# High parts of queries, keys and first weights fetched by casting DMAs on GpSimd instead of cast by ScalarE and VectorE

## The chip, the cores and the metric

The kernel runs on one core of a Trainium2 chip. The metric is the device time of one execution in microseconds (us). The engines are TensorE (PE, with its weight loads shown apart as PEld), VectorE (DVE), ScalarE (ACT), GpSimd (POOL) and SyncE (SP), which here only issues transfers.

## What is computed

Three layers follow one another; this is the reference cut to what matters.

```
# attention: q, k, v of [2, 8, 576, 64], f of [2, 8, 576]
scores = q @ k.T / 8 ; decay = cum[:, None] - cum[None, :]   # cum = cumsum(log f)
attn = softmax(where(causal, -1e9, scores + decay)) ; x = attn @ v     # x: [1152, 512]
# soft mixture of 8 experts with Sinkhorn-normalised P
out = sum_e P[:, e] * (relu(x @ w1[e]) @ w2[e])
# last layer
h = out @ w_in ; g = h * tanh(softplus(h)) ; result = g @ w_out
```

## The kernel before, in words

TensorE multiplies fp32r operands, which are rounded fp32. To keep precision, an operand is split into a high part (rounded to fp32r) and a low part (the fp32 value minus the high part), and a product is the sum of three matmuls: high by high, high by low, low by high.

**The attention stage.** The two batches have five query tiles each (ten tiles, `ti` 0 to 9), and each tile has four units of two heads (`pi` counts units, 0 to 39). The main loop runs over half-steps `s`; `pi = s // 2`, `a = s % 2`, and inside a tile `st` counts its units, so that a place in the loop is written `(st, a)`. What an engine does follows the order in which the loop emits it; nothing is reordered later. In a half-step come, in this order: the exponentials of the half-unit before (ACT), at `a = 1` the normalisation of the unit before (POOL, line 512), the scores of this half-unit (PE lines 468 and 469, then a masked reduction on DVE, line 481), a few warming matmuls, `fill()` (matmuls of the first expert once they are possible), at `a = 1` the product with v for the unit three back (PE line 568) and the transposes of the unit two back (PE lines 532 and 544), and then the preparation of the next tile.

**Preparation of the next tile (`prep`).** At `(0, 0)` the query tile `ti + 1` is split, at `(0, 1)` the key tile. Their four groups of transposes (PE line 361) are emitted at `(1, 0)`, `(1, 1)`, `(2, 0)` and `(2, 1)`, queries and keys in turn. The raw tile (`raw`, three buffers) was fetched by SP (`load_raw`, line 147) about a tile earlier. The split writes a tile `hl` (a ring of two buffers): high part by `split2` on ACT (line 317) or DVE (line 319), low part on DVE or POOL (line 321). Tile 1 has its `hl` inside `big`, the space that later holds the first expert's weights.

**The planner.** `pick` adds up costs per engine in `busy` and gives a piece of work to the engine that would be least loaded; POOL starts at 10000. Evictions from PSUM (`evac`, lines 307 to 313), the splits and the weight splits go by it.

**First weights.** At `pi = 7` SP starts to fetch the first half of the first expert (line 61); from `pi = 12` on one task a unit splits one of its eight 128x512 pieces: `split_w`, high part on ACT (line 325) or DVE (line 327), low part on DVE (line 329).

After the attention stage come the Sinkhorn steps, the experts and the last layer. The change touches nothing there.

Of the kernel before, what the change touches and what calls it, by code (L numbers as in the profile page):

```python
# [9 lines left out]
FR = mybir.dt.float32r  # L10
AF = mybir.ActivationFunctionType
ALU = mybir.AluOpType
# [4 lines left out]
B, H, S, D = 2, 8, 576, 64  # L17
# [9 lines left out]
QT = {  # L27
    0: [(0, 128), (128, 128), (256, 128), (384, 128), (512, 64)],
    1: [(0, 64), (64, 128), (192, 128), (320, 128), (448, 128)],
}  # L30
KTL = [(0, 128), (128, 128), (256, 128), (384, 128), (512, 64)]
# [7 lines left out]
def f(ap):  # L39
    return ap.bitcast(F32)  # L40
# [43 lines left out]
def attention_moe_kernel(  # L84
# [13 lines left out]
    nc = tc.nc  # L98
# [18 lines left out]
    first_w = {n: big[:, 2048 * i:2048 * (i + 1)] for i, n in enumerate(("w1h", "w1l", "w2h", "w2l"))}  # L117
# [11 lines left out]
    with ExitStack() as actx:  # L129
        ap1 = actx.enter_context(tc.tile_pool(name="ap1", bufs=1))  # L130
        rawp = actx.enter_context(tc.tile_pool(name="rawp", bufs=3))
        hlp = actx.enter_context(tc.tile_pool(name="hlp", bufs=2))
# [100 lines left out]
        def cumulate_b(lo, hi):  # L233
# [21 lines left out]
            out=mask, in_=mask, compare_op=ALU.is_ge, fill=NEG, base=512,  # L255
# [19 lines left out]
        def quads(t):  # L275
            return t.rearrange("p (u a) (z t) -> p u (a z) t", a=2, z=2)
# [19 lines left out]
        def spent(engine, ns):  # L296
            busy[engine] += ns

        def pick(**cost):
            e = min(cost, key=lambda k_: busy[k_] + cost[k_])  # L300
            busy[e] += cost[e]
            return e
# [12 lines left out]
        def split2(raw, hi, lo):  # L315
# [4 lines left out]
            eng = nc.vector if pick(dve=640, pool=1260) == "dve" else nc.gpsimd  # L320
            eng.tensor_tensor(out=lo, in0=raw, in1=f(hi), op=ALU.subtract)

        def split_w(raw, hi, lo):
            if pick(act=540, dve=360) == "act":
                nc.scalar.copy(out=hi, in_=raw)
            else:
                nc.vector.tensor_copy(out=hi, in_=raw)
            spent("dve", 640)
            nc.vector.tensor_tensor(out=lo, in0=raw, in1=f(hi), op=ALU.subtract)

        def duplicate(o, i):
            nc.sync.dma_start(out=f(o), in_=f(i))

        def prep(kind, b, i, slots):

            s0, n = QT[b][i] if kind == "q" else KTL[i]
            st = {}

            def split(half=None):
                if not half:  # L340
                    st["raw"] = raws.pop((kind, b, s0))
                    if (b, i) == (0, 1):
                        o = 1024 * (kind == "k")
                        st["hl"] = big[:, o:o + 1024].rearrange("p (h z d) -> p h z d", z=2, d=D)
                    else:
                        st["hl"] = hlp.tile([128, H, 2, D], FR, tag="hl", name="hl")
                raw, hl = st["raw"], st["hl"]
                hs = slice(0, H) if half is None else slice(4 * half, 4 * half + 4)
                z = 0 if kind == "q" else 1
                hi, lo = hl[:n, hs, z, :], hl[:n, hs, 1 - z, :]  # L350
                if half is None:
                    split2(raw[:n], hi, lo)
                else:
                    nc.scalar.copy(out=hi, in_=raw[:n, hs])
                    nc.vector.tensor_tensor(out=lo, in0=raw[:n, hs], in1=f(hi), op=ALU.subtract)

            def trans(g, early=False):
                hl = st["hl"]
                pt = ps_t.tile([128, 4, 128], FR, tag="pt", name="pt")
                for u in range(4):  # L360
                    nc.tensor.transpose(  # L361
                        out=pt[:, u, :n],
                        in_=hl[:n, 4 * g + u].rearrange("p a d -> p (a d)"),
                        identity=idr[:n, :n],
                    )
                hs = slice(4 * g, 4 * g + 4)
                pv = f(pt[:, :, :n])
                if kind == "q":
                    a_, b_ = qa[slots[g]], qb[slots[g]]
                    if n == 64:  # L370
                        evac(quads(a_)[:, :, 0:4:3], pv.rearrange("p (u z) t -> p u z t", z=2), 4 * n, 0.125)
                    else:
                        evac(a_[:, :, :n], pv, 4 * n, 0.125)
                    if early:
                        evac(b_[0:64, :, :n], pv[0:64], 4 * n, 0.125)
                    else:
                        duplicate(b_[0:64], a_[0:64])
                        if g:
                            cum_q(b, i, g, slots[g])
                else:  # L380
                    o = kbase[b] + s0
                    evac(kt[:, hs, o:o + n], pv, 4 * n)
                    if early:
                        evac(kb[0:64, hs, o:o + n], pv[64:128], 4 * n)
                    else:
                        duplicate(kb[0:64, hs, o:o + n], kt[64:128, hs, o:o + n])

            return split, trans
# [271 lines left out]
        tiles = [(b, i) for b in range(B) for i in range(len(QT[b]))]  # L660
        units = []
        for ti, (b, i) in enumerate(tiles):
            s0, n = QT[b][i]
# [39 lines left out]
        for s in range(2 * nu + 8):  # L703
            pi, a = divmod(s, 2)
            ti, st = divmod(pi, 4)
            live = pi < nu
            prepping = live and ti + 1 < len(tiles)
            if prepping and st == 0 and a == 0:
                (qs, qt_), (ks, kt_) = make_preps(ti + 1)
            if 1 <= s <= 2 * nu:  # L710
                expo(units[(s - 1) // 2], (s - 1) % 2)
            if a and 1 <= pi <= nu:
                normalize(units[pi - 1])
            if live:
                scores(units[pi], a)
            if s < 16:
                warm((2,2,2,2,2,2,2,2,1,1,1,1,1,1,1,1)[s])
            elif s in (17,19,21,25,27):
                warm_late(1)
            fill()  # L720
            fills += ready
            ready = []
            if a and 3 <= pi < nu + 3:
                w = units[pi - 3]
                attend(w)
                if w["h"] == H - 2 and w["ti"] in (2, 6, 9):
                    c = (2, 6, 9).index(w["ti"])
                    gates.append(c)
                    if c < 2:
                        ready.append(filler(c))  # L730
                elif gates:
                    logits.append(gate(gates.pop(0)))
            elif logits:
                gate_end(*logits.pop(0))
            if a and 2 <= pi < nu + 2:
                transposes(units[pi - 2])
            if first:
                first.pop(0)()
            if prepping:
                nb_, ni = tiles[ti + 1]  # L740
                if (st, a) == (0, 0):
                    if ti == 3:
                        pad(2)
                    elif ti == 4:
                        pad(1)
                    elif ti in (5, 6):
                        unpad(0 if ti == 5 else 2)
                    cum_q(nb_, ni, 0, (2 * ti + 2) % 3)
                    qs()
                elif (st, a) == (0, 1):  # L750
                    ks()
                    if ti:
                        next_loads(ti + 2)
                elif (st, a) == (1, 0):
                    qt_(0)
                elif (st, a) == (1, 1):
                    if ti == 3:
                        pad(0)
                    elif ti == 5:
                        unpad(1)  # L760
                    kt_(0)
                    load_v(nb_, ni)
                elif (st, a) == (2, 0):
                    qt_(1)
                elif (st, a) == (2, 1):
                    kt_(1)
            if late_rows and s >= 2:
                late_rows.pop(0)()
            if a:
                continue  # L770
            s = pi
            if s == 3:
                nc.gpsimd.tensor_copy(out=wgc[:, :, 0, :], in_=wg)
                nc.gpsimd.tensor_tensor(out=wgc[:, :, 1, :], in0=wg, in1=f(wgc[:, :, 0, :]), op=ALU.subtract)
            if s == 7:
                wts.load(0, 0, stage)
                wts.load(0, 1, stage)
            if s == 8:
                cum_k(1, 0, 256)
            if s == 22:  # L780
                cum_k(1, 256, 576)
            if s >= 12 and wtasks:
                wtasks.pop(0)()
# [399 lines left out]
    for g in range(NF):  # L1183
        half, gg = g // 4, g % 4
        ph = l1(half, gg, 2, ps_h)
        h = new_h()
# [374 lines left out]
    for n_, (c, kk) in enumerate((c, kk) for c in (1, 2) for kk in range(KD)):  # L1561
        b = TB[n_ % 2] if n_ > 3 else 5
# [20 lines left out]
    for u in range(12):  # L1583
        c, gg = divmod(u, 4)
        b = HB[u % 4]
# [192 lines left out]
    for p in range(13):  # L1778
# [10 lines left out]
        if p % 2 == 0 and p:  # L1789
            h, n = 17 + (p // 2 - 1) // 2, (p // 2 - 1) % 2  # L1790
# [94 lines left out]
```

## Time and profile before

| | |
|---|---|
| median of 3 runs | 1086.73 us (1086.53 to 1086.83) |
| the profiled execution | 1087.39 us |
| its span, first to last instruction | 1085.6 us |
| PE busy | 1078.3 us (99%) |
| DVE, ACT, POOL busy | 839.3, 542.3, 75.5 us |
| mean granted TensorE clock | 0.998 |

The busy time of PE includes matmuls that wait in its pipeline, so 99% does not say that PE is never late. Weight loads (964.5 us) and the chain of waits show more. POOL's busy time all lies in the first 160 us, which is the attention stage; transfers that an engine issues are not counted as busy.

### The profile page before, as it was taken

The page shows a single profiled execution, that of the slowest core. Times are in us where ns is not written, and L with a number is a line of the kernel's source. Part 1 is how long each engine was busy: PE and PEld are TensorE (multiplying, and loading weights), DVE is VectorE, ACT ScalarE, POOL GpSimd, SP SyncE. Part 2 cuts the span into 40 slices and gives each one's busy share as a digit, 9 for nine tenths or more (in the row PEclk, how much of TensorE's full clock was granted, in tenths as well). Part 3 has the DMA queues.
Part 4 walks back from the last instruction along what each step waited for, and adds up shares of the span by engine and source line. Part 5 has one row for each costly group of instructions (what it writes and reads, how often), then busy time and mean ns, then how long its engine had stood idle before and what let it go on. Part 6 is the DMA issues. An engine that isn't in the chain of part 4 may idle for free.

```text
span 1085.6 us, 18374 instructions
## 1 busy us (share of the span) xinstructions
PE 1078.3 (99%) x6838; PEld 964.5 (89%) x6838; DVE 839.3 (77%) x1891; ACT 542.3 (50%) x1287; POOL 75.5 (7%) x124
## 2 busy tenths in 40 slices
PE   9999999999999999999999999999999999999998
PEld 8788779998989899898989989899898989899997
DVE  7856647878797887977888796887977559788994
ACT  7756632354425243342624435253443458887881
POOL 6644420000000000000000000000000000000000
PEclk9999999999999999999999999999999999999999
DMA  6534202023241424425343342524322341161402
GB/s 147 140 93 105 74 21 78 1 98 102 94 145 68 151 78 150 136 89 155 99 154 96 119 149 95 158 85 146 124 96 83 129 155 42 65 207 60 162 1 88
DMA packets 103805, 114.98 MB, mean 106 GB/s; under 512 B 35236, under 2 KB 63860, under 8 KB 103716
## 3 DMA queue, kind: packets, MB, share of 16 engines
q1 hardware_dynamic: 103716, 113.81, 33.3%
q8 instruction: 54, 0.88, 0.3%
q14 instruction: 35, 0.29, 0.1%
HBM read 82.24 MB, written 27.07 MB: 101 GB/s over the span
## 4 chain that ended last, share of the span: by engine, by line
PE 97%; DVE 1%; ACT 0%; issue 0%; POOL 0%; DVEq 0%; POOLq 0%
PE bank L856 33%; PE bank L1266 29%; PE bank L1738 9%; PE bank L1648 4%; PE ph L826 3%; PE x L568 3%; PE spare L1648 2%; PE bank L1577 2%; PE pa L856 2%; PE pa L641 2%; PE ph L622 1%; PE sp L468 1%; PE pt L361 1%; PE pt L532 1%; PE wt L395 1%; PE sp L469 1%
## 5 line engine op out<-in xcount | busy, mean ns | idle before, releaser
L856 PE MATMUL bank<-w2h,big 128*128 128x512 f32 x924 | 296.7, 390 | 0.0
L856 PE MATMUL bank<-w2l,big 128*128 128x512 f32 x528 | 205.7, 390 | 0.0
L856 PEld LDWEIGHTS bank<-w2h,big 128*128 128x128 f32 x924 | 173.5, 188 | 36.0 <-DVE hid_b L834 0.2
L1295 ACT COPY snap<-bank 128x288 f32<-128x288 f32 x168 | 66.9, 398 | 167.5 <-PE bank L1266 165.2
L833 ACT ACTIVATE big<-c 128x288 fp32r<-128x288 f32 x168 | 75.1, 447 | 84.6 <-DVE c L1300 81.0
L856 PEld LDWEIGHTS bank<-w2l,big 128*128 128x128 f32 x528 | 99.1, 188 | 19.9
L834 DVE SCALAR_TENSOR_TENSOR big<-c,big 128x288 fp32r<-128x288 f32 x140 | 64.1, 458 | 56.8 <-ACT big L833 54.2
L1031 DVE SCALAR_TENSOR_TENSOR acc<-bank,P,acc 128x512 f32<-128x512 f32 x132 | 92.4, 747 | 15.7 <-PE bank L856 15.6
L1266 PE MATMUL bank<-tt,ss 128*128 128x288 f32 x672 | 103.0, 295 | 0.0
L1266 PE MATMUL bank<-xh,ss 128*128 128x288 f32 x448 | 102.7, 295 | 0.0
L1266 PEld LDWEIGHTS bank<-tt,ss 128*128 128x128 f32 x672 | 93.1, 188 | 0.2
L1300 DVE TENSOR_TENSOR c<-bank,snap 128x288 f32<-128x288 f32 x168 | 76.0, 452 | 18.7 <-PE bank L1266 18.5
L1012 ACT CAST hb<-da 128x512 fp32r<-128x512 f32 x38 | 23.8, 625 | 107.0 <-DVE da L987 95.9
L1266 PEld LDWEIGHTS bank<-xh,ss 128*128 128x128 f32 x448 | 76.4, 188 | 0.0
L1266 PE MATMUL bank<-xl,ss 128*128 128x288 f32 x224 | 66.1, 295 | 0.0
L1266 PE MATMUL bank<-xh,w1l 128*128 128x288 f32 x224 | 66.0, 295 | 0.0
L1266 PE MATMUL bank<-xl,w1h 128*128 128x288 f32 x224 | 65.9, 294 | 0.0
L1266 PE MATMUL bank<-xh,w1h 128*128 128x288 f32 x224 | 65.7, 293 | 0.0
L75 DVE TENSOR_TENSOR w2l<-stg,w2h 128x512 fp32r<-128x512 f32 x60 | 41.2, 690 | 13.6 <-ACT w2h L74 13.6
L856 PE MATMUL bank<-w2h,hid_b 128*128 128x512 f32 x132 | 51.4, 389 | 0.0
L512 POOL TENSOR_SCALAR p<-p,rs 128x256 f32<-128x256 f32 (+5 forms) x72 | 42.2, 596 | 65.7 <-DVE rs L508 44.5
L1266 PE MATMUL bank<-tt,w1h 128*128 128x288 f32 x224 | 46.0, 293 | 0.0
(314 smaller groups left out, 2464.0 us busy)
## 6 DMA issues: line engine op xcount, KB each, us to landing
stg<-in_moe_w_dram SPq DMA_DIRECT2D x64, 512.0 KB
wb<-w_in_b SPq DMA_DIRECT2D x42, 256.0 KB
raw<-in_moe_w_in_dram SPq DMA_DIRECT2D x16, 512.0 KB
raw<-in_moe_w_out_dram SPq DMA_DIRECT2D x16, 512.0 KB
w_in_b<-hb SPq DMA_DIRECT2D x18, 256.0 KB
w_out_h<-hb SPq DMA_DIRECT2D x16, 256.0 KB
w_out_l<-da SPq DMA_DIRECT2D x16, 256.0 KB
w_in_f<-da SPq DMA_DIRECT2D x12, 256.0 KB
```

Source lines behind the costliest of these rows:

```text
L75: (lo_engine or nc.vector).tensor_tensor(out=lo, in0=raw, in1=f(hi), op=ALU.subtract)
L512: nc.gpsimd.tensor_scalar(out=p[:n, a, :nk], in0=p[:n, a, :nk], scalar1=r[:n, a:a + 1], scalar2=1.0, op0=ALU.mult, op1=ALU.mult,)
L568: nc.tensor.matmul(out=x[64 * a:64 * a + 64, h // 2, :n], lhsT=vts[b, j][:w, h + a, :], rhs=pT[:w, 128 * j + 64 * a:128 * j + 64 * a + 64] ...
L833: nc.scalar.activation(out=hh, in_=ph, func=AF.Relu)
L834: nc.vector.scalar_tensor_tensor(out=hl, in0=ph, scalar=0.0, in1=f(hh), op0=ALU.max, op1=ALU.subtract)
L856: nc.tensor.matmul(out=pa, lhsT=a_[:, ts_], rhs=w[wn][ft_], start=(first and n == 0), stop=(last and n == 2),)
L1031: nc.vector.scalar_tensor_tensor(out=acc[t], in0=pa, scalar=P[:, t, e:e + 1], in1=acc[t], op0=ALU.mult, op1=ALU.add)
L1266: nc.tensor.matmul(out=by_chunk(out_) if len(v_.shape) == 3 else out_, lhsT=u, rhs=v_, start=first and m == 0, stop=m == 5, skip_group_che ...
L1295: nc.scalar.copy(out=t, in_=bank["x", g])
L1300: nc.vector.tensor_tensor(out=t, in0=bank[of, g], in1=snap[with_, g], op=ALU.add)
L1648: nc.tensor.matmul(out=out_, lhsT=a_(kk, pa), rhs=b_(kk, pb), start=first and q == 0, stop=q == 5, skip_group_check=True,)
L1738: nc.tensor.matmul(out=bk[b][:, cs], lhsT=a_[:, ts_], rhs=w[wn][i][:, cs], start=i == 0 and q == 0, stop=i == 3 and q == 2,)
```

## The change

For tiles 2 to 9 the high parts of queries and keys no longer come from the raw tile on chip. A transfer issued by GpSimd reads the same rows from device memory a second time and rounds them to fp32r on the way into `hl`. It is issued two tiles ahead: the query's at `(2, 1)` and the key's at `(3, 0)` of tile `ti` for tile `ti + 2`. The low part is still a subtraction at the old place. The first expert's first weights get their high parts likewise, by four GpSimd transfers at `pi` 4, 5, 6 and 7. The raw tiles are fetched as before.

```diff
+        def lo_half(raw, hi, lo):
+            eng = nc.vector if pick(dve=640, pool=1260) == "dve" else nc.gpsimd
+            eng.tensor_tensor(out=lo, in0=raw, in1=f(hi), op=ALU.subtract)
+
+        high = {}
+
+        def load_high(kind, ti):
+            b, i = tiles[ti]
+            s0, n = QT[b][i] if kind == "q" else KTL[i]
+            t = hlp.tile([128, H, 2, D], FR, tag="hl", name="hl")
+            nc.gpsimd.dma_start(
+                out=t[:n, :, 0 if kind == "q" else 1],
+                in_=(q if kind == "q" else k)[b, :, s0:s0 + n, :].rearrange("h p d -> p h d"),
+            )
+            high[kind, b, i] = t
+
+        def load_high_w(part):
+            kk = part % 2
+            src = w1[0, kk * 256:(kk + 1) * 256, :512] if part < 2 else w2[0, kk * 256:(kk + 1) * 256, :]
+            nc.gpsimd.dma_start(
+                out=first_w["w1h" if part < 2 else "w2h"][:, 1024 * kk:1024 * kk + 1024].rearrange("p (k n) -> p k n", k=2),
+                in_=src.rearrange("(k p) n -> p k n", p=128),
+            )
+
         def split_w(raw, hi, lo):
-            if pick(act=540, dve=360) == "act":
-                nc.scalar.copy(out=hi, in_=raw)
-            else:
-                nc.vector.tensor_copy(out=hi, in_=raw)
             spent("dve", 640)
             nc.vector.tensor_tensor(out=lo, in0=raw, in1=f(hi), op=ALU.subtract)
...
+                    elif (kind, b, i) in high:
+                        st["hl"] = high.pop((kind, b, i))
+                        lo_half(st["raw"][:n], st["hl"][:n, :, 0 if kind == "q" else 1], st["hl"][:n, :, 1 if kind == "q" else 0])
+                        return
...
+            if live and ti + 2 < len(tiles) and (st, a) in ((2, 1), (3, 0)):
+                load_high("k" if a == 0 else "q", ti + 2)
...
             s = pi
+            if 4 <= s < 8:
+                load_high_w((2, 3, 0, 1)[s - 4])
```

## Rows read from the trace of the kernel before

**Rows 1.** Windows: busy time per engine, clock, share and rate of transfers.

```profile
20.00:40.00 20.00, 19.69 (x187) 16.32 (x187) 15.79 (x59) 17.21 (x49) 11.57 (x20) 1.00 0.65 175
...
400.00:800.00 400.00, 400.00 (x2345) 362.60 (x2345) 329.45 (x652) 161.15 (x364) 0.00 (x0) 1.00 0.39 125
```

**Rows 2.** Chain that ended last, 26 to 50 us: start, length, what.

```profile
39.84 0.33 DVE hl L319
40.18 0.35 DVE big L327
...
40.55 1.65 DVE big L329
```

**Rows 3.** Waits of weight loads, 17 to 50 us: total, times, longest.

```profile
PEld pt L361 <- POOL hl L321: 1.3, 3, 0.6
PEld sp L468 <- DVE nmax L481: 1.0, 1, 1.0
```

**Rows 4.** Windows of 4 us; the granted clock is third from the end.

```profile
42.00:46.00 4.00, 3.08 (x32) 2.43 (x31) 3.48 (x12) 2.52 (x6) 2.40 (x3) 0.78 0.44 99
46.00:50.00 4.00, 4.00 (x42) 2.73 (x40) 2.87 (x10) 3.03 (x8) 2.33 (x5) 0.80 0.65 182
```

**Rows 5.** Groups by line, 17 to 116 us: busy us, mean ns, idle before.

```profile
L319 DVE CAST hl<-raw 128x512 fp32r<-128x512 f32 x9 | 7.3, 808 | 0.0
...
L327 DVE CAST big<-stg 128x512 fp32r<-128x512 f32 x4 | 1.7, 420 | 0.0
...
L325 ACT CAST big<-stg 128x512 fp32r<-128x512 f32 x4 | 2.5, 621 | 0.0
...
L317 ACT CAST hl<-raw 128x512 fp32r<-128x512 f32 x3 | 1.8, 612 | 0.0
```

**Rows 6.** POOL in order of time: start, length, idle before and its releaser.

```profile
16.34 0.72 POOL L512 TENSOR_SCALAR p<-p,rs 128x128 f32<-128x128 f32 x2 [1.43 <-DVE rs L508]
...
17.81 0.72 POOL L512 TENSOR_SCALAR p<-p,rs 128x128 f32<-128x128 f32 x2 [0.26 <-DVE rs L508]
...
24.89 0.93 POOL L512 TENSOR_SCALAR p<-p,rs 128x256 f32<-128x256 f32 x2 [1.15 <-ACT p L493]
27.74 0.94 POOL L512 TENSOR_SCALAR p<-p,rs 128x256 f32<-128x256 f32 x2 [1.91 <-PE pt L544]
29.10 1.28 POOL L321 TENSOR_TENSOR hl<-raw,hl 128x512 fp32r<-128x512 f32 x1 [0.43 <-ACT hl L317]
...
35.50 1.15 POOL L512 TENSOR_SCALAR p<-p,rs 128x384 f32<-128x384 f32 x2 [1.66 <-DVE rs L508]
38.14 1.15 POOL L512 TENSOR_SCALAR p<-p,rs 128x384 f32<-128x384 f32 x2 [1.49 <-DVE rs L508]
...
40.26 1.39 POOL L321 TENSOR_TENSOR hl<-raw,hl 64x512 fp32r<-64x512 f32 x1 [0.47 <-DVE hl L319]
```

**Rows 7.** PE in order of time, what reads those tiles.

```profile
19.81 0.44 PE L544 MATMUL pt<-idn,p 128*128 128x128 f32 x2
...
20.61 0.51 PE L361 MATMUL pt<-idr,hl 128*128 128x128 f32 x4
...
29.12 0.66 PE L544 MATMUL pt<-idn,p 128*128 128x128 f32 x4
...
35.70 0.54 PE L361 MATMUL pt<-idr,hl 128*128 128x128 f32 x4
```

**Rows 8.** SP and DVE at the start: a load's issue and its reader.

```profile
0.74 0.40 SPq L199 DMA_DIRECT2D cum<-in_f_dram  x1
...
2.53 0.74 DVE L216 TENSOR_SCALAR cum<-cum 16x576 f32<-16x576 f32 x1 [0.52 <-DMA cum<-in_f_dram]
```

**Rows 9.** Line 147, SP's raw loads: min/median/max ns of the issue.

```profile
L147 SPq DMA_DIRECT2D raw<-in_q_dram x8: 394/398/671, 8.0 to 97.6; - x8
```

**Rows 10.** DVE in order of time, the low part of tile 2's queries.

```profile
19.77 0.69 DVE L321 TENSOR_TENSOR hl<-raw,hl 128x512 fp32r<-128x512 f32 x1
```

**Rows 11.** Waits of POOL, 0 to 163 us: total, times, longest.

```profile
POOL p L512 <- DVE rs L508: 44.5, 24, 4.3
```

## The prediction

> **What bounds the kernel now.** I began with the windows. From 400 to 800 us the weight loads are busy 362.6 of 400 us and PE all of it; between 20 and 40 us it is 16.3 of 20, while DVE and ACT are busy 15.8 and 17.2 [rows 1]. The change touches nothing behind the attention stage, and that long part is PE's own work, so the question is only how much later or earlier the attention stage ends; whatever PE loses there is not made up afterwards. Next I read the chain of waits from 26 to 50 us for places where it leaves PE: around 40 us it runs through two of the removed casts and a low part of 1.65 us on DVE [rows 2]. The view of waits prices this: weight loads waited 1.3 us for the low parts that POOL writes (line 321), and 1.0 us for DVE's reduction [rows 3]. Then the clock: it is 0.78 and 0.80 in two windows of 4 us behind those waits, that is 4 x 0.22 + 4 x 0.20 = 1.7 us of full-speed time [rows 4]. So the most that the removal can give is 1.3 + 1.0 + 1.7 = 4.0 us, though 24 casts of 0.4 to 0.8 us each go away. Nearly all of these lie beside PE's work. The last view is POOL's timeline with PE's readers beside it [rows 6, 7], for the new work goes on POOL's queue.
>
> **The change part by part.**
>
> *Removed.* 16 high parts of tiles and 8 of weights: 12 and 4 on DVE, 4 and 4 on ACT; means 0.81 and 0.42 us on DVE, 0.61 to 0.62 on ACT [rows 5], about 16 us of work. I worked the planner's sums through with the costs in the code: the low parts stay where they were (14 of 18 on POOL) and three evictions change engine, which I cost at nothing, since both engines have idle time [rows 1]. Of the casts only those near 29 and 40 us delay PE. The low part at 29.10 waited 0.43 us for ACT's cast, the one at 40.26 waited 0.47 us for DVE's [rows 6]. At 39.84 the two casts (0.33 and 0.35 us on the chain) put DVE's weight subtraction at 40.55, beside POOL's low part at 40.26, and it took 1.65 us [rows 2, 6]; a tile subtraction of the same shape took 0.69 [rows 10]. Without the casts it starts before POOL's, and the 1.0 us wait for DVE goes [rows 3].
>
> *Added: POOL's time for a transfer.* The trace of before has none. A tile's high part is 128 partitions x 8 heads = 1024 pieces of 256 bytes. Lower end: SP issues the same pattern in 0.40 us [rows 9]. Upper end: POOL's low part of 512 elements takes 1.28 us, 2.5 ns an element [rows 6]; one such step for each of 1024 pieces makes 2.6 us (four words for each, 10 us, is an outer bound). I take T = 1.28 us, the POOL instruction of the same tile. A weight transfer has 256 pieces: 0.40 to 0.64 us; I take 0.64. The Trainium skill ("DMA: Bandwidth & Descriptors", Anatomy of one DMA) says that generating descriptors is a small part and that many can be emitted before it shows; no run here shows it yet, and by it T would be near the lower end and the sum about -3 us.
>
> *Added: what queues behind it.* POOL has 20 more instructions, all in its one queue with the normalisations, whose results PE reads one unit later. Where POOL's idle time and the reader's slack cover them they are free:
> - Tile 2, behind the normalisation at 16.34: 0.26 us idle before 17.81, and its result, ready at 18.53, is read at 19.81, 1.28 later [rows 6, 7]. Covered 1.54, needed 2T = 2.56: 1.0 us late.
> - First three weight transfers: each falls in its own gap (1.15 us before 24.89 is one) [rows 6] and needs 0.64: nothing.
> - Tile 3 and the fourth weight transfer, behind 25.82: 1.91 us idle before 27.74, result ready at 28.68, read at 29.12, 0.44 later [rows 6, 7]. Covered 2.35, needed 2.56 + 0.64 = 3.2: 0.85 us late. The low part that waited 0.43 us for ACT now waits as long for POOL: no gain there.
> - Tile 4, behind 36.65: 1.49 us idle before 38.14 [rows 6]; 2.56 makes POOL 1.07 late. The low part at 40.26 no longer waits 0.47, so it is 0.6 later.
> - Tiles 5 to 9: POOL idles up to 4.3 us before a normalisation [rows 11]; 2.56 fits: nothing at this T, and several us in all at twice of it.
>
> The buffer of `hl` that a transfer writes is freed by transposes a half-step earlier. For tile 4 these are at 35.70, before POOL gets there at 36.65 [rows 6, 7], so that this new wait costs nothing; were it late, the next normalisation would stand behind it.
>
> *Added: landing.* The low parts now wait for a transfer. The lower end is 1.8 us, the 36 KB load issued at 0.74 and read at 2.53 after a wait for it [rows 8]. A tile has 256 KB; at the 175 GB/s moved from 20 to 40 us [rows 1] that adds 1.5 us, so 1.8 to 3.3. Tile 2's query transfer is issued at about 17.06; with T it lands between 20.1 and 21.6, where DVE began the low part at 19.77, in order ahead of its reductions [rows 10]. It ended at 20.46 and PE read it at 20.61 [rows 7]. PE is 0.2 to 1.7 us late; this overlaps the 1.0 above, and I take 1.2 for both. SP's queue keeps all it had. The extra bytes (3.7 MB for tiles, 2.1 MB for weights) fall between 17 and 110 us, over half of them before 40, where transfers are already at 0.65 [rows 1]: between nothing (the duplicates are read half a tile later) and 1 us for tile 3's landing; I take 0.3.
>
> *The sum.* 1.2 (tile 2) + 0.85 (tile 3) + 0.3 (crowding) + 0.6 (tile 4's low part) - 1.0 (DVE's wait) - 0.8 (half of the 1.7 us of clock, since PE still waits at 40 us, but less) = +1.15 us. On the profiled execution's 1087.39 (span 1085.6 and 1.8 around it) that makes 1088.5; the runs shown have a median of 1086.73, 0.66 below the profiled one, so 1087.9.
>
> **The rivals.** A measurement of this kernel can tell about 0.2%, 2.2 us, from no change.
>
> *Faster: POOL issues as quickly as SP.* With T = 0.40 all POOL gaps cover the transfers. Tile 2's landing costs about 0.4, and tile 3 gains 0.3, tile 4's wait 0.4, DVE's 1.0 and the clock 1.7: -3.0, 1083.7; without the landing and with all waits gone, -4.0, 1082.7. For it speaks SP's row, against it that POOL's rows are all slower. It decides below T of about 0.55.
>
> *Slower: POOL becomes the bound of the early tiles.* One mechanism: PE's transposes wait for normalisations queued behind transfers. By the same three places, the sum reaches +2.2 at T = 1.6. At T = 2.56: 3.6 (5.12 - 1.54), 3.4 (5.76 - 2.35), 3.1 for tile 4 (3.6 less the 0.47), 1.5 for tile 5, 4 for the four others, less 1 of gains: +14.6, 1101. At 10 us, in the outer bound, eight pairs of some 20 us would each exceed their gaps by 15 and the kernel would lose 100 us. For it: the slack is 0.4 to 1.5 us at the early places [rows 6, 7]. Against: later gaps are long [rows 11].
>
> *Slower: DVE and POOL hold each other up.* DVE's subtraction took 1.65 us beside POOL's, against 0.69 [rows 2, 10]. If transfers were held by DVE's work in this way, each of the nine before 45 us would last 1.0 longer: T = 2.3, about +11, 1098. The Trainium skill ("SBUF — State Buffer", Who interferes with whom) says that descriptor writing is blocked by DVE's copies and casts in two-port modes, not by subtractions; the trace shows a subtraction held by POOL, but cannot show the rule itself. By it the change takes most of the blockers away.
>
> *The change does less than it says.* If a transfer did not round, low parts would be zeros and nothing would be faster or slower: this gives no other time.
>
> **How the numbers follow.** T between 0.55 and 1.6, gains against early delays: 0.37, 1084.6 to 1088.9, with 1087.9 as its time. Faster: 0.22. Slower, T from 1.6 to 2.6 or DVE's hold: 0.28, 1088.9 to 1101. Beyond: 0.13. The range for 8 in 10 runs from 1083.5 (about 0.05 lies below) to 1101 (0.13 above). That makes faster 0.22, same 0.37, slower 0.41.
>
> **What would show it.** In the profile after: POOL's transfer instructions between normalisations, about 1.3 us each; the normalisation of 17.81 about a us later and PE's transposes behind it late; DVE without lines 319 and 327 beyond tile 1; no wait of line 468 near 43 us; the end of the attention stage, by the first matmul of line 826, within 2 us of before. I would be wrong if POOL's transfers last under 0.5 or over 1.6 us, if low parts wait for landings in later tiles too (rounding on the way may be slow, which no row shows), or if the clock falls at another place.

## The result and the profile after

The changed kernel takes 1093.52 us (median of 11 runs, 1090.83 to 1096.19), beside it the kernel before 1086.84 us (11 runs, 1086.53 to 1092.02). The ratio is 1.0052, with an interval of 1.0038 to 1.0066: half a per cent, or 6.7 us, slower. That lies in the predicted range and 5.6 us above the predicted time. The profiled execution took 1096.18 us, its span 1094.3 us, 8.7 us longer than before; it is a long one of the 11.

All of it is lost in the attention stage. The first matmul of the expert stage (line 826 before, 854 after) is at 163.2 us before and at 172.0 us after, 8.8 us later, and the long part behind it is as it was:

```profile
L826 PE MATMUL ph<-xh,big x32: 333/334/422, 163.2 to 176.3; 128*128 128x384 f32 x32
```

```profile
L854 PE MATMUL ph<-xh,big x32: 333/334/422, 172.0 to 185.1; 128*128 128x384 f32 x32
```

These windows of the changed kernel answer to [rows 1] (us, then the busy time of PE, PEld, DVE, ACT and POOL, the granted clock, the share of transfers, which adds up the time of all packets in flight and can exceed 1, and their rate):

```profile
20.00:40.00 20.00, 17.97 (x140) 15.16 (x142) 11.50 (x46) 12.76 (x37) 13.45 (x22) 0.83 1.31 292
400.00:800.00 400.00, 400.00 (x2335) 362.08 (x2334) 330.66 (x656) 161.52 (x365) 0.00 (x0) 1.00 0.39 124
```

Between 20 and 40 us DVE is busy 4.3 us less and ACT 4.5 us less, but PE too is busy 1.7 us less, at a clock of 0.83. Transfers take twice their former share. POOL in order of time, against [rows 6]:

```profile
16.32 0.72 POOL L536 TENSOR_SCALAR p<-p,rs 128x128 f32<-128x128 f32 x2 [1.44 <-DVE rs L532]
16.98 1.11 POOL L333 DMA_DIRECT2D hl<-in_q_dram  x1
18.09 0.88 POOL L333 DMA_DIRECT2D hl<-in_k_dram  x1
...
19.52 0.72 POOL L536 TENSOR_SCALAR p<-p,rs 128x128 f32<-128x128 f32 x2
20.19 0.78 POOL L342 DMA_DIRECT2D big<-in_moe_w_dram  x1
...
30.69 0.87 POOL L333 DMA_DIRECT2D hl<-in_k_dram  x1 [1.07 <-PE pt L385]
31.55 0.70 POOL L342 DMA_DIRECT2D big<-in_moe_w_dram  x1
```

A tile's transfer holds POOL for 0.69 to 1.11 us, one of the weights for 0.70 to 0.78. The normalisation that began at 17.81 begins at 19.52, but what PE then waits for is something else. DVE (first two rows) and PE (last two) at tile 2, against [rows 7, 10]:

```profile
21.60 0.69 DVE L325 TENSOR_TENSOR hl<-raw,hl 128x512 fp32r<-128x512 f32 x1 [2.23 <-DMA hl<-in_q_dram]
24.30 0.69 DVE L325 TENSOR_TENSOR hl<-raw,hl 128x512 fp32r<-128x512 f32 x1 [1.41 <-DMA hl<-in_k_dram]
```

```profile
22.39 0.51 PE L385 MATMUL pt<-idr,hl 128*128 128x128 f32 x4 [1.31 <-DVE rs L528]
25.09 0.72 PE L385 MATMUL pt<-idr,hl 128*128 128x128 f32 x4 [0.65 <-DVE hl L325]
```

The low part that began at 19.77 begins at 21.60, because the transfer issued at 16.98 has only then landed, and PE's transposes come at 22.39 in place of 20.61. (The name after the first PE wait is the instruction that DVE ran next; the tile that PE reads is the one of 21.60.) The chain, against [rows 2], says the same, and shows a second place:

```profile
17.04 1.05 POOL hl L333
18.09 6.19 DMA hl<-in_k_dram
24.30 0.70 DVE hl L325
...
36.34 8.62 DMA qb<-qa
44.96 0.65 issue
45.61 0.76 PE sp L493
```

At 45 us the scores wait for duplicates, copies within the chip that SP issues and that the change does not touch. That of the queries (`qb`), issued at 36.34, takes 8.62 us to land. The 0.65 us that the chain calls "issue" is most likely that of the keys (`kb`): SP issued it at 38.55, and the last semaphore event of its landing is at 45.51. The wait for DVE of [rows 3] is gone, as are all casts of [rows 5] but tile 1's; a wait of 2.1 us for the duplicates stands in its place. And the clock, against [rows 4]:

```profile
24.00:31.00 7.00, 6.35 (x36) 5.56 (x35) 4.08 (x15) 4.10 (x13) 3.92 (x8) 0.52 0.98 266
45.00:55.00 10.00, 9.39 (x57) 7.00 (x59) 5.52 (x15) 3.20 (x8) 5.29 (x8) 0.50 0.41 92
```

Behind each wait PE runs at the lower of its two levels, for some 7 and some 10 us.

### The profile page after: what moved, and what is told of

Its sections match the earlier page's. It is cut to its first block, busy times and chain, and to the rows that moved or that the text cites. A ratio compares the mean times of both kernels' runs of the same rounds, so it can differ in the third digit from the quotient of the medians.

```text
span 1094.3 us, 18411 instructions
## 1 busy us (share of the span) xinstructions
PE 1084.1 (99%) x6838; PEld 968.8 (89%) x6838; DVE 830.1 (76%) x1876; ACT 536.9 (49%) x1278; POOL 89.8 (8%) x144
## 3 DMA queue, kind: packets, MB, share of 16 engines
q0 software_dynamic: 15680, 5.77, 3.5%
## 4 chain that ended last, share of the span: by engine, by line
PE 96%; DMA 2%; DVE 1%; issue 1%; POOL 0%; ACT 0%; DVEq 0%; POOLq 0%; ACTq 0%
PE bank L884 33%; PE bank L1294 28%; PE bank L1766 9%; PE bank L1676 4%; PE ph L854 3%; PE x L592 2%; PE spare L1676 2%; PE bank L1605 2%; PE pa L884 2%; PE pa L665 1%; PE ph L646 1%; PE sp L492 1%; PE pt L385 1%; PE pt L556 1%; DMA qb<-qa 1%; PE sp L493 1%
## 5 line engine op out<-in xcount | busy, mean ns | idle before, releaser
L505 DVE CUSTOM_DVE_ANT_0 p<-sp,mask 128x256 f32<-128x256 f32 (+4 forms) x64 | 32.1, 501 | 20.0 <-PE sp L493 17.6
```

The costliest lines, as they stand in the source:

```text
L505: nc.vector.tensor_tensor_reduce(out=p[:n, a, o:o + w], in0=t[:n, :w], in1=mask[:n, m0 + o:m0 + o + w], scale=-1.0, scalar=prev, op0=ALU.a ...
```

## One account for all runs

Over 20 to 60 us two things are read from one window of each trace: PE's idle time (40 less its busy time) and what the clock costs (40 times one less the granted clock). The row of before, and that of the changed kernel:

```profile
20.00:60.00 40.00, 38.74 (x376) 30.35 (x377) 31.58 (x103) 29.75 (x78) 22.67 (x37) 0.96 0.54 144
```

```profile
20.00:60.00 40.00, 35.70 (x286) 28.43 (x287) 23.11 (x80) 23.86 (x66) 24.82 (x41) 0.79 0.93 207
```

Before: 1.3 idle and 1.6 for the clock, 2.9 us. After: 4.3 and 8.4, 12.7 us, 9.8 more, beside a span that is 8.7 longer. The rows of all kernels, worked out alike (profiled spans; ratios to the kernel before with their intervals; in the last column the lowest and the highest mean granted clock of the kernel's executions, over the whole span):

| kernel | median us | ratio | idle + clock, less 2.9 | span less 1085.6 | clock of its executions |
|---|---|---|---|---|---|
| the change | 1093.52 | 1.0052 (1.0038 to 1.0066) | 4.3 + 8.4: +9.8 | +8.7 | 0.992 to 0.998 |
| tiles_only | 1092.28 | 1.0052 (1.0034 to 1.0070) | 3.6 + 3.6: +4.3 | +4.3 | 0.995 to 0.998 |
| weights_only | 1088.83 | 1.0014 (1.0000 to 1.0028) | 3.6 + 1.6: +2.3 | +4.4 | 0.997 to 1.000 |
| traffic_round | 1093.08 | 1.0050 (1.0031 to 1.0070) | 6.0 + 0: +3.1 | +4.5 | 0.993 to 1.000 |
| traffic_plain | 1094.93 | 1.0057 (1.0034 to 1.0079) | 5.9 + 5.2: +8.2 | +10.0 | 0.993 to 1.000 |
| pool_stall | 1092.19 | 1.0043 (1.0025 to 1.0061) | 3.7 + 5.2: +6.0 | +5.5 | 0.993 to 1.000 |
| tiles_4_on | 1093.72 | 1.0053 (1.0037 to 1.0070) | 3.1 + 8.0: +8.2 | +7.9 | 0.992 to 0.998 |
| tile2_early | 1094.65 | 1.0071 (1.0054 to 1.0087) | 6.8 + 3.6: +7.5 | +6.2 | 0.995 to 0.998 |
| weights_late | 1086.02 | 0.9983 (0.9970 to 0.9996) | 0.7 + 0: -2.2 | -1.3 | 0.999 to 1.000 |
| tiles_warm | 1094.33 | 1.0056 (1.0037 to 1.0076) | 4.5 + 1.6: +3.2 | +5.7 | 0.997 to 1.000 |
| spread | 1087.45 | 0.9997 (0.9985 to 1.0009) | 2.0 + 0: -0.9 | -0.3 | 0.999 to 1.000 |
| late_both | 1085.51 | 0.9983 (0.9973 to 0.9994) | 1.9 + 0: -1.0 | -0.8 | 0.999 to 1.000 |
| all_moved | 1089.54 | 1.0023 (1.0014 to 1.0031) | 3.4 + 1.6: +2.1 | +3.6 | 0.995 to 1.000 |

The account follows the spans to about 2.5 us (idle time outside the window, and eight warming matmuls more in tiles_warm, are not in it). In these profiles the change and five of the twelve experiments lost more to the lower clock than the kernel before, three lost as much (1.6 us), and four lost nothing.

One profile is not the whole of a kernel, though. Of the 84 executions of the kernel before beside the experiments, 51 have a mean clock of 0.999 or 1.000 (median 1086.7 us), 21 have 0.998 (1087.4 us; the profiled one is of this kind), and 12 have 0.993 to 0.995 (1091.6 us): the same program loses 5 us in some executions, and the clock is low in these. The change's profiled execution has the lowest clock of its 11. The one with the median time has 0.997, which over its span of 1091.6 us makes about 3.3 us (an estimate), half of its loss. traffic_round kept the full clock in its profile, but has 0.993 to 0.998 in its eight other executions. weights_late, spread and late_both, the three that are not slower than the kernel before, kept 0.999 or 1.000 in every one of 12 executions. Nor is the clock all of it: the six executions of tiles_only at 0.998 took 1090.06 to 1097.29 us.

## The experiments

**tiles_only** and **weights_only**: each half of the change alone.

Weights cast on chip:

```diff
-            if 4 <= s < 8:
-                load_high_w((2, 3, 0, 1)[s - 4])
...
+            if pick(act=540, dve=360) == "act":
+                nc.scalar.copy(out=hi, in_=raw)
+            else:
+                nc.vector.tensor_copy(out=hi, in_=raw)
```

> The tile transfers alone: the four weight transfers are gone and the weights' high parts are cast on ScalarE and VectorE as before. Theory A (the transfers are late because they and SP's transfers crowd the same span, the 2.1 MB of weights most of all): the landings of tiles 2 to 4 fall from 4.6 to 6.3 us towards the 4.0 us of the quiet stretch from 75 to 125 us, SP's duplicate of queries that landed 8.6 us after its issue is back near 3 us, the wait at 45 us goes, and only the wait for tile 2's landing stays: 1087.5 to 1090 us. Theory B (POOL's queue is the bound, 16 of the 20 issues remain): 1091.5 to 1093.5 us. Theory C (rounding makes each transfer slow whatever else runs): landings stay at 4.6 us and over, 1091 to 1093 us.

1092.28 us, the number of theories B and C alike; theory A expected less, so the weights' bytes are not what makes most of the loss. Three windows show tile 2 alone:

```profile
20.00:23.00 3.00, 1.33 (x9) 0.98 (x10) 1.04 (x4) 0.38 (x2) 0.23 (x1) 0.98 1.58 254
23.00:30.00 7.00, 7.00 (x39) 5.78 (x38) 3.08 (x16) 4.82 (x13) 4.01 (x7) 0.52 0.52 122
30.00:60.00 30.00, 28.05 (x288) 21.66 (x287) 24.87 (x71) 21.48 (x57) 21.53 (x34) 1.00 0.81 171
```

PE is idle for 1.7 of 3 us, then busy for 7 us without a gap and at half clock, which costs another 3.4 us. DVE waited 2.6 us for tile 2's query here, and there is no second such stretch.

Tiles cast on chip:

```diff
-            if live and ti + 2 < len(tiles) and (st, a) in ((2, 1), (3, 0)):
-                load_high("k" if a == 0 else "q", ti + 2)
```

> The four weight transfers alone: tiles are cast on chip as before. Theory A: nothing waits for their landing (they are read 10 us later), but SP's duplicates and raw loads between 20 and 45 us land later: 1087 to 1090 us, with a wait of PE for a duplicate. Theory B: 4 issues of 0.75 us fit POOL's gaps, and two casts near 40 us are gone: 1084.5 to 1086.8 us. Theory C: nothing waits for a landing, as B.

1088.83 us, as A expected. The chain gives the place:

```profile
23.85 7.01 DMA kb<-kt
30.86 0.14 issue
31.00 0.42 PE sp L493
```

A duplicate took 7.01 us to land (in the trace of before the last semaphore event of a duplicate comes 2.1 to 3.8 us after its issue, from 14 to 60 us), PE stood 3.2 us for it, and the clock was 0.66 from 31 to 36 us. The wait and the low clock of [rows 3, 4] between 42 and 50 us are gone. (Of the span's +4.4, some 2 us come between 240 and 860 us, where all kernels run the same code; the median is the better guide.)

**traffic_round** and **traffic_plain**: the kernel before with the same 5.8 MB fetched by GpSimd at the same places into idle accumulators; nothing reads them and all casts stay. The weights come in eight halves, so that POOL issues 24 transfers and not 20. The second fetches fp32 without rounding (no `.bitcast(FR)`).

```diff
+            t = acc[3 if kind == "q" else 4].bitcast(FR)
+            nc.gpsimd.dma_start(out=t[:n].rearrange("p (h d) -> p h d", d=D), in_=...)
```

> The kernel before with all its casts, and beside them the extra reads alone: the same rounding transfers at the same places, written to accumulators that nothing reads (the weights in eight halves). Theory A: no low part waits for a landing, crowding stays: 1088 to 1091 us, with late duplicates near 40 us. Theory B: POOL's issues delay normalisations as in the changed kernel and no cast is gone: 1092 to 1095 us. Theory C alone, without crowding: as before, 1086.5 to 1088 us.

> As the run before, but the extra transfers copy fp32 without rounding. Theory C (rounding is what makes them slow): landings fall from over 4 us to some 3 us and the time to 1086.5 to 1088 us, clear of the rounding run. Theories A and B: landings within 0.5 us of the rounding run's and a time within 1 us of it.

1093.08 and 1094.93 us, 1.9 us apart, but not clear of each other by their intervals: without anything that reads what lands, the loss is there, and without rounding too. Theory C falls; the first is the number of B and above that of A. The queue rows of 17 to 125 us (packets, MB, share of the engines) show that rounding is not free all the same, first with, then without:

```profile
q0 software_dynamic: 15744, 5.77, 37.9%
```

```profile
q0 software_dynamic: 1792, 5.77, 18.4%
```

With rounding the same bytes cost twice the engines' time and come in nine times as many packets; yet PE's waits are alike. With rounding the longest up to 45 us are these (PE in order of time):

```profile
20.72 0.68 PE L560 MATMUL pt<-idn,p 128*128 128x128 f32 x2 [0.88 <-POOL p L528]
29.91 0.42 PE L485 MATMUL sp<-kb,qb 96*128 96x384 f32 x1 [0.82 <-DMA kb<-kt]
...
44.00 0.47 PE L485 MATMUL sp<-kb,qb 96*128 96x512 f32 x1 [2.15 <-DMA qb<-qa]
```

0.88 us is POOL's queue; 0.82 and 2.15 us are duplicates that land late beside the extra traffic. Without rounding the longest are 0.67 us for POOL's queue, and 0.72 and 1.82 us for the duplicates.

**pool_stall**: POOL's time alone, with no byte moved. A place held 1.1 us, a transfer's 0.7 to 1.1.

```diff
+        def stall():
+            for _ in range(2):
+                nc.gpsimd.memset(acc[5], 0.0)
...
+            if live and ti + 2 < len(tiles) and (st, a) in ((2, 1), (3, 0)):
+                stall()
...
+            if 4 <= s < 8:
+                stall()
```

> The kernel before with two memsets (about 1.0 us of POOL's time together) at each of the 20 places where the change issues a transfer; nothing is fetched and all casts stay. Theory A (transfers land late and crowd the others; POOL's own time is covered): within 1 us of before, 1086 to 1088, and no clock drop at 24 to 31 us. Theory B (the normalisations queue behind POOL's issues): 3 to 6 us slower, 1090 to 1093, with PE waiting for POOL's normalisation of tile 0 and 1.

1092.19 us: theory B's number, A's fails here. PE waited 0.88 us for the normalisation behind the first two stalls, and 0.83 us for another ahead of 31.08; from 20 to 45 us its clock stayed at 1.00. It fell behind two later waits, 0.60 us for a low part of POOL ahead of 44.59 and 0.92 us for DVE's reduction ahead of 46.01, of which the kernel before has the second too. From 45 us it was 0.56 and from 50 to 60 us 0.71:

```profile
45.00:50.00 5.00, 4.08 (x33) 3.25 (x31) 3.82 (x13) 2.04 (x5) 3.48 (x5) 0.56 0.47 93
50.00:60.00 10.00, 10.00 (x74) 7.05 (x74) 6.24 (x18) 6.00 (x15) 5.42 (x12) 0.71 0.31 88
```

The executions tell the two apart. With the times that POOL was held for (2.27, 3.44 and 2.27 us), the prediction's three places give 0.73 + 1.09 + 0.78 = 2.6 us late. Three of the seven executions, at a clock of 0.999 or 1.000, are 2.4 to 2.7 us over the median of before beside them (1087.01); the four at 0.993 to 0.997 are 5.2 to 7.9 us over it.

So POOL's time alone, at somewhat more a place than the change takes, costs 5.2 us, the tiles' transfers alone 5.4, traffic that nobody reads 6.2 and 8.1, and the change with all of it 6.7: the causes don't add up. That was the reason for a theory D: an early stall costs its own 1 to 3 us, and the clock behind it the rest.

**tiles_4_on**: tiles_only, but tiles 2 and 3 keep their casts.

```diff
-            if live and ti + 2 < len(tiles) and ...
+            if live and 4 <= ti + 2 < len(tiles) and ...
```

> Only tiles 4 to 9 get their high parts by GpSimd's transfers; tiles 2 and 3 and the weights keep their casts. Theory A (tile 2's transfers, issued at 17 to 18 us, land after DVE wants them): the loss of tiles_only (5.4 us) goes, 1086 to 1088. Rival (every tile loses a part of it, for late landings or for POOL's queue): six of eight tiles are left, so 1089.5 to 1092.

1093.72 us, as much as with all eight tiles and above the rival's 1092: theory A fails again. Before 38 us the trace is that of before. Then tile 4 is the first (POOL in order of time):

```profile
38.54 0.91 POOL L333 DMA_DIRECT2D hl<-in_q_dram  x1 [1.94 <-PE pt L560]
39.45 0.69 POOL L333 DMA_DIRECT2D hl<-in_k_dram  x1
40.17 1.65 POOL L540 TENSOR_SCALAR p<-p,rs 128x384 f32<-128x384 f32 x2
...
43.35 1.26 POOL L325 TENSOR_TENSOR hl<-raw,hl 64x512 fp32r<-64x512 f32 x1 [1.03 <-DMA hl<-in_q_dram]
```

POOL stood idle for 1.94 us before the first transfer, and the normalisation that began at 38.14 in [rows 6] stood behind it until 40.17. (The profile names a transpose of PE, but those that read this `hl` are over by 36.2; what POOL waited for stays open.) The low part came at 43.35 in place of 40.26, PE's weight loads waited 2.2 us for it, and from 44 to 60 us the clock was 0.50.

**tile2_early**: as tiles_only, with tile 2's transfers at the half-steps 2 and 3.

```diff
+            if s in (2, 3):
+                load_high("kq"[s == 2], 2)
```

> As tiles_only, with tile 2's two transfers issued four half-steps earlier (both before the second unit's end); all else of the tiles as in the change, weights cast on chip. Theory A (landing of tile 2 alone): most of the 5.4 us come back, 1087 to 1089; what is left is crowding of tile 1's duplicates. Rival (POOL's time for tiles 2 and 3, or landings of later tiles): 1090 to 1093 as before.

1094.65 us, above what either expected. Tile 2 no longer stalls, as A says; tile 3 does instead:

```profile
37.81 0.75 PE L389 MATMUL pt<-idr,hl 128*128 128x128 f32 x4 [4.18 <-POOL hl L325]
```

Its key transfer, issued at 26.21, landed only before 36.49, where POOL began the low part after 4.4 us idle. These 10.2 us are the longest of any tile transfer in a kernel that reads them; SP issued its two weight loads of 512 KB at 26.59 and 27.25, right behind it.

**weights_late**: as weights_only, with one transfer at each of the units 9, 11, 13 and 15, in the order of use.

```diff
+            if s in (9, 11, 13, 15):
+                load_high_w((s - 9) // 2)
```

> As weights_only, but the four transfers are issued at units 9, 11, 13 and 15 in the order of use, three units ahead of their readers. Theory A (weights_only lost what it gained because its transfers delayed a duplicate that PE waited for at 31 us): the wait at 31 us goes and 1.5 to 2.5 us are gained over weights_only, 1085.0 to 1087.0. Rival (the weights' casts were hidden, nothing is to be gained): 1086.5 to 1089 with a wait at the new place.

1086.02 us, ratio 0.9983 (0.9970 to 0.9996): a small gain, as A expected. No wait for a duplicate, and the clock is full from 20 to 60 us. DVE's first weight subtraction, 1.65 us long beside POOL's in [rows 2], now comes 0.5 us earlier and takes 0.68:

```profile
40.06 0.68 DVE L349 TENSOR_TENSOR big<-stg,big 128x512 fp32r<-128x512 f32 x1
```

**tiles_warm**: tiles_only with eight warming matmuls in PE's gap.

```diff
                 elif (st, a) == (1, 0):
+                    if ti == 1:
+                        warm(8)
                     qt_(0)
```

> tiles_only (1092.3 us) with eight more warming matmuls (about 1.7 us) on PE just ahead of tile 2's first transposes, where PE stood idle for 1.6 us at 21 us and its clock then fell to half until 30 us. Theory D (the stall itself costs about 2 us, the clock that falls behind it the other 3): PE stays busy, the clock stays full, and tile 2 costs the stall alone, 1087.5 to 1089.5. Rival (the 5.4 us are the waits themselves, the clock only follows): 1092 to 1094.

1094.33 us, not the 1087.5 to 1089.5 of theory D, and just above the rival's 1092 to 1094. The windows say why:

```profile
20.00:25.00 5.00, 4.66 (x39) 3.97 (x40) 2.30 (x9) 1.46 (x5) 0.94 (x3) 1.00 1.21 208
25.00:30.00 5.00, 4.17 (x41) 3.69 (x42) 3.29 (x15) 4.28 (x13) 3.48 (x6) 1.00 0.47 108
35.00:40.00 5.00, 3.52 (x29) 2.96 (x27) 2.01 (x8) 2.82 (x8) 2.39 (x3) 0.90 0.76 210
40.00:45.00 5.00, 5.00 (x55) 3.84 (x55) 3.42 (x11) 2.73 (x9) 2.78 (x5) 0.75 0.68 139
```

With its gap filled, the clock stays at 1.00 from 20 to 30 us, where tiles_only had 0.52 for 7 us: the clock does follow the idle time. But now tile 3's transfer stalls PE at 36 us, and the clock falls there. In tiles_only that wait was 0.42 us, for PE was some 5 us late by then; tile 3's key landed at 36.2 us there and at 36.5 us here, though it was issued 1.4 us earlier here. One loss thus covers the next.

**spread**: tiles_only with `hl` of tiles 2 to 4 in the unused part of `big`, and the transfers of tiles 2 to 5 three half-steps earlier; still 16 transfers on POOL.

```diff
+            if ti in (2, 3, 4):
+                o = 2048 * (ti - 1) + 1024 * (kind == "k")
+                t = big[:, o:o + 1024].rearrange("p (h z d) -> p h z d", z=2, d=D)
...
-            ... and (st, a) in ((2, 1), (3, 0)):
+            ... and (st, a) in (((1, 0), (1, 1)) if ti < 4 else ((2, 1), (3, 0))):
```

> tiles_only with the hl of tiles 2, 3 and 4 in the still unused part of the first weights' buffer, so that the transfers of tiles 2 to 5 wait for no buffer and are issued three half-steps earlier (tiles 6 to 9 as in the change); the same 16 transfers on POOL's queue. Theory L (the stalls come from late landings and from POOL standing before a buffer that is not free yet): 1086 to 1088.5, no DVE or POOL wait for a landing before 60 us. Theory P (POOL's issue time alone, as pool_stall showed): still one stall with a clock drop behind it, 1089.5 to 1093.

1087.45 us, ratio 0.9997 (0.9985 to 1.0009): 5 us of tiles_only's loss are gone, as L expected. The landings are as slow as ever (4.5 and 5.2 us for the 256 KB ones between 5 and 60 us), but nobody waits for them, and the clock stays full:

```profile
20.00:60.00 40.00, 38.03 (x380) 30.00 (x381) 30.32 (x99) 28.28 (x77) 27.99 (x45) 1.00 0.86 182
```

The transfers of tiles 2 to 5 have other places in POOL's queue here too, so that the gain of the earlier landing and that of the other place are not told apart.

**late_both**: transfers for tiles 6 to 9 only, and the weights as in weights_late.

```diff
-            if live and ti + 2 < len(tiles) and ...
+            if live and 6 <= ti + 2 < len(tiles) and ...
...
-            if 4 <= s < 8:
-                load_high_w((2, 3, 0, 1)[s - 4])
+            if s in (9, 11, 13, 15):
+                load_high_w((s - 9) // 2)
```

> The change with its transfers only where the traces show slack: tiles 6 to 9 (from about 62 us on) and the weights one at a time at units 9, 11, 13, 15. Theory D (one stall of some 2 us before 50 us plus the clock that falls behind it makes up the loss; later units are long enough to cover POOL and landings): 1085 to 1087, no slower than before and near weights_late's 1086.0. Rival (the first transferred tile always stalls PE, wherever it lies): 1088 to 1092 with a clock drop behind about 70 us.

1085.51 us, ratio 0.9983 (0.9973 to 0.9994), as D expected, the lowest median of all and 8 us below the change: it beats the kernel before by 0.2%, and so does weights_late, so that the tiles' part gained nothing more. PE waited 1.25 us ahead of 39.97 for a duplicate, with no low clock behind it.

**all_moved**: the whole change, with the edits of spread and weights_late together:

```diff
+            ... and (st, a) in (((1, 0), (1, 1)) if ti < 4 else ((2, 1), (3, 0))):
...
+            if s in (9, 11, 13, 15):
+                load_high_w((s - 9) // 2)
```

> The whole change (all 16 tile transfers and the four of the weights) with the places of spread and of weights_late together: hl of tiles 2 to 4 in the unused part of the first weights' buffer, tiles 2 to 5 issued three half-steps earlier, the weights one at a time at units 9, 11, 13 and 15. Theory L and D (the loss is one early stall of PE, by a late landing or a buffer not yet free, and the clock behind it; the transfers as such cost little): no stretch at half clock before 60 us, 1085.5 to 1088. Rival (5.8 MB more, wherever it falls, delays SP's duplicates until PE stands long enough once): 1089 to 1093, with a wait for a duplicate between 25 and 55 us and half clock behind it.

1089.54 us, ratio 1.0023 (1.0014 to 1.0031): the rival's number. PE at tile 3:

```profile
38.73 0.50 PE L496 MATMUL sp<-kt,qa 128*128 128x512 f32 x1
42.07 0.76 PE L497 MATMUL sp<-kb,qb 96*128 96x512 f32 x1 [2.83 <-issue]
```

The first matmul, with the originals, ran; the second, which differs only in reading the duplicates, came 2.83 us late. The profile names no releaser, but the last semaphore event of the keys' duplicate, issued by SP at 34.25, is at 41.98. From 42.07 to 44 us the clock was 0.50. Transfers were at a share of 1.64 from 35 to 40 us. Two sets of transfers that each fit alone don't fit together.

## Why the prediction missed by 5.6 us

The measured time lies in the stated range, and that is luck: the range's upper part was priced for a T of 1.6 to 2.6 us or for DVE holding POOL's transfers, and neither came. The two other signs that the text named as ways to be wrong did come: low parts waited for landings in later tiles too (2.20 us ahead of 46.94), and the clock fell at another place.

**POOL's time for a transfer: over-sized, and not the cause.** T was taken as 1.28 us; it is 0.69 to 1.11, and 0.70 to 0.78 for the weights (0.64 taken). By the prediction's own rule that points towards less loss, not more. The rule of the Trainium skill ("DMA: Bandwidth & Descriptors", Anatomy of one DMA) that many descriptors can be emitted before it shows agrees: a weight transfer with 256 pieces holds POOL for a median of 0.75 us, a tile's with 1024 for 0.87 to 0.95 behind the first (1.11), little more, and one of 64 rows, with 512, for 0.69 to 0.76. All are about twice SP's 0.40 of [rows 9]. (The text's sum for a T of 1.6 us is, by its own three places, +2.9 and not +2.2; nothing here hangs on it.)

**The places in POOL's queue: right.** Tile 2 was put at 2T less 1.54; pool_stall, with 2.27 us there, gives 0.73 by that formula, and PE waited 0.88. All three places give the loss of its executions at full clock.

**Landing: the first step that failed.** The prediction let a tile land in 1.8 to 3.3 us, from a 36 KB load and the mean rate. In the changed kernel the 16 tile transfers took 2.8 to 6.4 us from their issue, with a median of 4.5; four of them are of 64 rows, half the bytes. Tile 2's query was 4.60 us under way and its key 6.19. So PE was 1.8 us late at tile 2's first transposes, just above the "0.2 to 1.7" of the text, and waited another 0.65 us at the key's. The trace of before had a nearer row than the 36 KB load: SP's raw loads of the same rows, whose last semaphore event comes 2.9 to 4.2 us after the issue between 19 and 31 us. The fit of a DMA's time in the Trainium skill ("DMA: Bandwidth & Descriptors", Anatomy of one DMA) would give, as an estimate, about 2.6 us for 256 KB. No GpSimd transfer of 256 KB in these runs took less than 3.2 us, and the measurement decides.

**Crowding: under-sized.** 0.3 us was taken, between nothing and 1 us, since duplicates are read half a tile later. Duplicates took 2.1 to 3.8 us in the kernel before, 7.01 us in weights_only and 8.62 us in the change, and PE waited 3.2 and 2.1 us for them. SP's two weight loads issued ahead of the latter (31.70 and 32.36) took 9.1 and 11.1 us to their last semaphore event, where they took 4.5 and 5.3 before. The Trainium skill ("DMA: Bandwidth & Descriptors", Issuing engines are not separate DMA queues) states that transfers of all issuing engines run on the same transfer engines and interleave, and this agrees with it.

**The clock: the sign was wrong.** The sum gave back 0.8 us of [rows 4]. In the profiled execution after, the clock costs 8.4 us between 20 and 60 us where it cost 1.6, and that is most of that execution's loss; in the median execution it is about half. Nor was there 0.8 us to give back in most executions of the kernel before: [rows 4] are from one at 0.998, and 51 of 84 have 0.999 or 1.000. The text named a clock that "falls at another place" as a way to be wrong, but priced no stall with it. Behind a stall of 1.7 us in tiles_only came 7 us at 0.52, 3.4 us: the factor was about three.

**The gain: about right.** DVE's wait and half of the clock were put at -1.8 us together. weights_late shows it alone: its ratio of 0.9983 is -1.8 us (-3.3 to -0.4), the span is 1.3 shorter, the account to 60 us 2.2, and the subtraction that took 1.65 takes 0.68. Its 12 executions all kept the clock, where 12 of 84 before fell to 0.995 or less. The bound of 4.0 us was never reached.

**The rivals.** POOL as the bound showed in pool_stall and in traffic_round (0.88 us each at tile 2), about what the text's formula gives; in the change the landing came later than POOL's queue and covered it. DVE and POOL holding each other up did not show: no transfer of the change held POOL for over 1.11 us. Of the signs, "slower" had the greatest chance (0.41), but the forecast time stood in "same".

Still open: why the same stall is followed by a low clock in one kernel and not in another, and in one execution and not in another of the same kernel (late_both's 1.3 us at 40 us was not; the profiled execution of traffic_round lost its 6 us of idle time at full clock, eight others did not keep it), and how much of the change's 6.7 us belongs to each of the three causes, since each hides the others.

## What to carry to other kernels

Before work is moved to a transfer, ask what is read from it first and when it is issued, and count on the slowest landing beside the present traffic, for the transfers that are already there too. In a stage where TensorE is close to its suppliers, price a stall with the clock behind it, and expect one stall to hide the next: causes don't add up, and only a version without any early stall shows what the idea is worth (here 0.2%, from the weights' transfers, where there was slack; spread's 16 tile transfers, without a stall, gained nothing that shows). And take the clock from several executions, for one profile can be an extreme of its kernel.

## What was not expected of the hardware

Rounding on the way doubles the transfer engines' time per byte (37.9% against 18.4% for 5.77 MB; the rounding transfers have 15744 packets, the plain ones 1792, so that it may be the pieces as much as the rounding), and yet PE's waits and the time were no worse for it. Between 75 and 125 us, where traffic is light, a rounding transfer of 256 KB still took about 4 us from issue to landing (3.2 to 4.7). The plain ones of traffic_plain took as long there (3.4 to 5.5), so that it is not the rounding. SP's raw loads of the same rows in the same kernel, in the same pieces, had their last semaphore event 2.8 to 3.6 us after the issue; that GpSimd's way of issuing makes the difference is argued from these rows and was not tested by itself.
